# Loading the weights anew for every matmul of the modulation stage

## The chip, the cores and the metric

The kernel runs on one core of a Trainium2 chip. The metric is the device time of one execution, in microseconds (us), lower being better.

## The reference

A decode step of one transformer block for 8 sequences, one token each. The modulation is the first step: it gives six vectors of 1024 for each sequence. Attention over a cache of 8192 positions and a gated feed-forward layer follow.

```python
mod = (silu(c) @ w_mod).reshape(8, 6, 1, 1024)      # w_mod: 1024 x 6144, bf16, 12.6 MB
sa, ca, ga, sb, cb, gb = mod[:, 0], ..., mod[:, 5]
h = layernorm(x) * (1 + ca) + sa
x = x + ga * attention(h, k_cache, v_cache, wq, wo)  # K and V: 67 MB each; wq, wo: 8.4 MB each
h = layernorm(x) * (1 + cb) + sb
x = x + gb * reglu(h, W_gate, W_up, W_down)          # 7.3 MB each
```

## The kernel before

All large inputs stream through one ring in on-chip memory, in a fixed order: w_mod in two halves, wq in two halves, then K and V pieces by turns, then the rest. A load is issued as soon as the ring space that it needs has been read. The ring holds 16.8 MB, so the second half of wq needs the space of w_mod's first half, and the first K piece that of w_mod's second half. This is how the modulation can, in principle, hold up the stream.

```python
def hold(ins, when):                 # marks matmuls that shall not load weights
    if when:
        holding.append(ins)
    return ins
...
for i in range(2):                                   # the two halves of w_mod
    fns = []
    for kk in range(4 * i, 4 * i + 4):               # 8 slices of the contraction
        w = arena[:, ...]                            # [cut]
        for pr in range(3):                          # 3 pairs of output vectors
            for j in range(4):                       # 4 column tiles of the array
                fns.append(lambda e, ...: hold(e.matmul(
                    ps[32 * j:32 * j + 32, pr, :], hT[:, kk, :], w[:, 2 * pr:2 * pr + 2, j, :],
                    start=(kk == 0), stop=(kk == KC - 1), tile_position=(0, 32 * j)), pr > 0))
    P.op("pe", fns, reads=[R("hT"), slot_r(...)], writes=[bank(0, 3)])
```

The weights (the stationary operand) of all 12 matmuls of a slice are the same: `hT[:, kk, :]`, 128 rows by 32 columns. The four matmuls of a pair work side by side, each on its own 32 columns of the array; I call them a group. With `pr > 0` held, only the first group of a slice loads weights. The query projection and the gate/up matmuls hold theirs in the same way.

## Time and profile before

Median 436.92 us, 436.73 to 436.95 in three runs. The profiled execution has a span of 435.6 us.

The page's slices: each digit is the busy share, in tenths, of one of 40 equal slices of the span (10.9 us each); PEclk is the clock granted to TensorE, in tenths of full speed (below, "half clock" is 0.50); the last line is the data rate. The queue line gives packets, megabytes and the share of 16 engines' time.

```profile
PE   0415238659595958768595958768595958636437
...
PEclk9966668697888869696978969696987969668858
DMA  9999999999999999999999999999999999999995
GB/s 373 438 444 433 429 433 433 434 430 432 433 433 433 433 433 433 433 433 433 433 433 433 433 433 433 433 433 433 433 433 433 433 433 433 423 429 444 428 420 233
...
q1 hardware_dynamic: 6944, 185.61, 98.9%
```

The data engines are busy in every slice but the last, at a rate that hardly moves between the first and the last; TensorE (PE) is busy for at most half of each of the first four slices. The Trainium skill ("DMA: Bandwidth & Descriptors", Specifications) gives 435 GB/s as the ceiling of the fabric into on-chip memory; the 433 GB/s of this trace agree. The kernel is at that ceiling, so a change can make it slower only by interrupting the stream or by lengthening what follows the last data; the modulation stands at the start, where only the first can happen.

The modulation's line (L521) in the list by line: first its matmuls, then its weight loads (PEld), with count, shortest, median and longest duration in ns.

```profile
L521 PE MATMUL ps<-arena,hT x96: 378/634/635, 17.8 to 35.9; 128*32 128x512 bf16 x96
L521 PEld LDWEIGHTS ps<-arena,hT x32: 98/150/152, 17.8 to 35.1; 128*32 128x32 bf16 x32
```

The second half of the stage in the timeline (start, duration, engine, line, operation; in brackets the idle time before and what ended it), up to the first use of wq:

```profile
31.74 0.11 PEld L521 LDWEIGHTS ps<-arena,hT 128*32 128x32 bf16 x4 [10.37 <-DMA arena<-in_w_mod_dram]
31.74 4.54 PE L521 MATMUL ps<-arena,hT 128*32 128x512 bf16 x48 [9.24 <-DMA arena<-in_w_mod_dram]
32.57 0.16 PEld L521 LDWEIGHTS ps<-arena,hT 128*32 128x32 bf16 x4 [0.72 <-issue]
33.85 0.17 PEld L521 LDWEIGHTS ps<-arena,hT 128*32 128x32 bf16 x4 [1.11 <-issue]
35.13 0.16 PEld L521 LDWEIGHTS ps<-arena,hT 128*32 128x32 bf16 x4 [1.12 <-issue]
36.33 0.33 SPq L393 DMA_DIRECT2D arena<-in_A_k_cache_dram  x1
...
41.40 3.60 PE L544 MATMUL ps<-arena,hT 128*32 128x512 bf16 x32 [5.11 <-DMA arena<-in_A_wq_dram]
```

Four things are to be read here. TensorE waited 9.24 us for the data. The four loads of a slice overlap each other: four of a median 150 ns span 0.16 us. Slices follow each other every 1.28 us, which is three groups at 0.427 us. And the end of the stage releases the first K load at 36.33 us, while TensorE itself next waits 5.11 us for wq.

### The profile page before, as it was taken

How to read it: one execution, taken by the hardware profiler on the slowest of the kernel's cores; microseconds unless marked ns; L12 is line 12 of the kernel's file. 1: busy time of each engine (PE TensorE's matmuls, PEld its weight loads, DVE VectorE, ACT ScalarE, POOL GpSimd, SP SyncE). 2: the span in 40 equal slices, each digit the busy share in tenths (PEclk: the TensorE clock that was granted, in tenths of full speed). 3: DMA queues.
4: the chain of work that ended last, by engine and by line, in shares of the span. 5: the costliest groups of instructions: out<-in, count | busy, mean ns of one | idle time of the engine just before them, and what ended most of it. 6: DMA issues, size and time to landing. Idle time of an engine off the chain costs nothing.

```text
span 435.6 us, 3869 instructions
## 1 busy us (share of the span) xinstructions
PE 277.4 (64%) x1643; PEld 120.8 (28%) x1483; DVE 265.8 (61%) x377; ACT 29.9 (7%) x62; POOL 14.5 (3%) x32
## 2 busy tenths in 40 slices
PE   0415238659595958768595958768595958636437
PEld 0100002324242423324242333324142323334105
DVE  1503058777686877777778777677788776253020
ACT  2000010110101010010101010010101010110000
POOL 7000000000000000000000000000000000000000
PEclk9966668697888869696978969696987969668858
DMA  9999999999999999999999999999999999999995
GB/s 373 438 444 433 429 433 433 434 430 432 433 433 433 433 433 433 433 433 433 433 433 433 433 433 433 433 433 433 433 433 433 433 433 433 423 429 444 428 420 233
DMA packets 7078, 185.74 MB, mean 426 GB/s; under 512 B 832, under 2 KB 928, under 8 KB 1312
## 3 DMA queue, kind: packets, MB, share of 16 engines
q1 hardware_dynamic: 6944, 185.61, 98.9%
q8 instruction: 5, 0.08, 0.1%
q10 hardware_dynamic: 128, 0.04, 0.0%
q14 instruction: 1, 0.01, 0.0%
HBM read 185.63 MB, written 0.02 MB: 426 GB/s over the span
## 4 chain that ended last, share of the span: by engine, by line
PE 46%; DVE 20%; issue 13%; DMA 6%; ACT 0%; SPq 0%
PE ps L646 22%; PE ps L597 18%; DVE kt L586 9%; DMA arena<-in_B_W_down_dram 6%; DVE negm L609 5%; PE ps L615 2%; PE ps L663 2%; PE ps L743 1%; DVE om L657 1%; DVE mj L620 1%; PE ps L774 1%; DVE mjt L623 1%; DVE negm L613 1%; DVE kt L733 0%; DVE lx L706 0%
## 5 line engine op out<-in xcount | busy, mean ns | idle before, releaser
L586 DVE STREAM_TRANSPOSE kt<-arena 128x1024 uint32<-128x1024 uint32 x128 | 149.6, 1217 | 39.0 <-PE ps L597 26.8
L597 PE MATMUL ps<-kt,qpad 128*128 128x512 bf16 x512 | 122.4, 385 | 9.6 <-DVE kt L586 8.3
L646 PE MATMUL ps<-arena,pT 128*64 128x512 bf16 x512 | 95.4, 554 | 51.7 <-issue 51.7
L646 PEld LDWEIGHTS ps<-arena,pT 128*64 128x64 bf16 x512 | 45.5, 157 | 95.5 <-issue 91.1
L597 PEld LDWEIGHTS ps<-kt,qpad 128*128 128x128 bf16 x512 | 46.0, 97 | 84.6 <-DVE kt L586 28.7
L636 DVE STREAM_TRANSPOSE pT<-prb 64x1024 bf16<-64x1024 bf16 x32 | 39.6, 1239 | 18.1 <-ACT prb L629 17.6
L629 ACT ACTIVATE prb<-ps,bias 128x1024 bf16<-128x1024 f32 x16 | 17.8, 1113 | 293.1 <-DVE mjt L623 293.1
L609 DVE TENSOR_REDUCE negm<-ps 128x1 f32<-128x512 f32 x32 | 22.1, 692 | 12.7 <-PE ps L597 12.7
L663 PE MATMUL ps<-jmp,om 128*128 128x16 f32 x34 | 7.4, 293 | 17.0 <-DVE om L657 17.0
L657 DVE SCALAR_TENSOR_TENSOR om<-ps,im,om 128x128 f32<-128x128 f32 x51 | 17.7, 347 | 0.7
L615 PE MATMUL ps<-identf,negm 128*128 128x128 f32 x32 | 7.8, 326 | 15.6 <-DVE negm L613 15.6
L578 POOL TENSOR_TENSOR qpad<-qR,mq 128x128 bf16<-128x128 bf16 x16 | 6.3, 399 | 317.6 <-DVE pT L636 267.7
L774 PE MATMUL ps<-arena,hT 128*32 128x448 bf16 x128 | 9.4, 459 | 9.4 <-DMA arena<-in_B_W_up_dram 6.8
L544 PE MATMUL ps<-arena,hT 128*32 128x512 bf16 x64 | 7.1, 623 | 12.7 <-DMA arena<-in_A_wq_dram 12.7
L521 PE MATMUL ps<-arena,hT 128*32 128x512 bf16 x96 | 9.2, 565 | 9.2 <-DMA arena<-in_w_mod_dram 9.2
L793 PE MATMUL ps<-arena,hmT 128*32 128x256 bf16 x112 | 8.7, 320 | 5.6 <-DMA arena<-in_B_W_down_dram 5.4
L528 DVE COPY mod<-ps 128x512 f32<-128x512 f32 x2 | 1.3, 671 | 17.8 <-PE ps L521 17.8
L781 DVE TENSOR_TENSOR kt<-ps,kt 128x448 bf16<-128x448 f32 x2 | 1.2, 621 | 17.6 <-PE ps L774 17.6
L663 PEld LDWEIGHTS ps<-jmp,om 128*128 128x128 f32 x34 | 5.7, 210 | 20.5 <-DVE om L657 20.5
L615 PEld LDWEIGHTS ps<-identf,negm 128*128 128x128 f32 x32 | 4.7, 187 | 23.6 <-DVE negm L613 23.6
L555 DVE CAST kt<-ps 128x512 bf16<-128x512 f32 x1 | 0.7, 692 | 16.3 <-PE ps L544 16.3
L793 PEld LDWEIGHTS ps<-arena,hmT 128*32 128x32 bf16 x112 | 6.2, 114 | 9.0 <-DMA arena<-in_B_W_down_dram 7.6
(89 smaller groups left out, 89.2 us busy)
## 6 DMA issues: line engine op xcount, KB each, us to landing
arena<-in_A_k_cache_dram SPq DMA_DIRECT2D x16, 4096.0 KB, 21.1
arena<-in_A_v_cache_dram SPq DMA_DIRECT2D x16, 4096.0 KB, 19.0
arena<-in_A_wq_dram SPq DMA_DIRECT2D x2, 4096.0 KB, 34.9
arena<-in_A_wo_dram SPq DMA_DIRECT2D x2, 4096.0 KB, 18.0
arena<-in_B_W_gate_dram SPq DMA_DIRECT2D x2, 3584.0 KB, 15.5
arena<-in_B_W_up_dram SPq DMA_DIRECT2D x2, 3584.0 KB, 19.0
arena<-in_w_mod_dram SPq DMA_DIRECT2D x1, 6144.0 KB, 30.7
arena<-in_w_mod_dram SPq DMA_DIRECT2D x1, 5888.0 KB, 16.6
```

The source lines that it names most:

```text
L521: fns.append(lambda e, w=w, pr=pr, j=j, kk=kk: hold(e.matmul(ps[32 * j:32 * j + 32, pr, :], hT[:, kk, :], w[:, 2 * pr:2 * pr + 2, j, :], s ...
L586: P.op("dve", lambda e: e.transpose(ktb[:, to:to + QE].bitcast(dt.uint32), arena[:, lo:lo + QE].bitcast(dt.uint32)), reads=[slot_r(lo, lo ...
L597: fns.append(lambda e, t=t, r=r: e.matmul(ps[:, b, :].rearrange("p (c k) -> p c k", k=32), qpad[:, m % 2, t * 2 + r, 24 - 8 * i:152 - 8 * ...
L609: P.op("dve", lambda e: e.tensor_reduce(negm[:, h:h + 1], ps[:, b, :], AX.X, ALU.max, negate=True), reads=[bank(b)] + (free(("v", m - 1)) ...
L615: P.op("pe", lambda e: e.matmul(ps[:, 4, 0:128], negm[:, 2:3].to_broadcast([128, 128]), identf[:], start=True, stop=True), reads=[R("negm" ...
L629: P.op("act", lambda e: e.activation(prb[:], ps[:, 2 * z:2 * z + 2, :].rearrange("p h n -> p (h n)"), ACT.Exp, bias=bias[:, z:z + 1], scal ...
L636: P.op("dve", lambda e, g=g: e.transpose(pT[64 * g:64 * g + 64, z, :, g, :], prb[64 * g:64 * g + 64, :]), reads=[R("prb")] + ([R("qpad", z ...
L646: fns.append(lambda e, t=t: e.matmul(ps[64 * (t % 2):64 * (t % 2) + 64, 5, :].rearrange("p (i d) -> p i d", d=Dh), pT[:, z, t].rearrange(" ...
L657: P.op("dve", lambda e, i=i: e.scalar_tensor_tensor(out=om[:], in0=ps[:, 5, Dh * i:Dh * i + Dh], scalar=im[:, i:i + 1], in1=om[:], op0=ALU ...
L663: P.op("pe", lambda e: e.matmul(ps[:, 6 + z, 0:16], om[:], jmp[:].rearrange("p g j -> p (g j)"), start=True, stop=True), reads=[R("om"), R ...
L774: fns.append(lambda e, w=w, r=kk - r0, kk=kk, h=h, j=j, b0=b0: hold(e.matmul(ps[32 * j:32 * j + 32, b0 + h, 0:H], hT[:, kk, :], w[:, r, j, ...
L793: fns.append(lambda e, w=w, r=k - r0, k=k, i2=i2, j=j: e.matmul(ps[32 * j:32 * j + 32, 4, 0:256], hmT[:, k, 1 - i2:33 - i2], w[:, r, i2, j ...
```

## The change

The intent: every one of the modulation's 96 matmuls loads its weights, 64 loads more than before. Nothing else changes; on each engine the order of instructions is the same.

```diff
-                            start=(kk == 0), stop=(kk == KC - 1), tile_position=(0, 32 * j)), pr > 0))
+                            start=(kk == 0), stop=(kk == KC - 1), tile_position=(0, 32 * j)), False))
```

## The prediction

> **What bounds the kernel now.** Data movement. The page's slices show the 16 DMA engines at least 90% busy in 39 of 40 slices, mostly at 433 GB/s; the input queue alone takes 98.9% of 16 engines' span (queue table), for 185.6 MB. TensorE matmuls cover 64%, VectorE 61%. In the modulation stage (first 37 us) TensorE is mostly idle: it waits 9.2 us for the second half of w_mod (waits).
>
> **What the change does.** Each of 8 slices of the contraction does 3 output pairs x 4 column tiles of 128x512 matmuls, 96 in all. Before, only the first pair loads weights: 32 loads of 128x32 (median 150 ns; four together span 0.16 us in the timeline). After, all 96 load: 64 more loads; nothing is removed or re-ordered. The query and gate/up matmuls keep their held weights.
>
> **Cost on TensorE.** 16 more groups of four, 16 x 0.16 = 2.6 us of weight-load busy time, nearly all hidden under running matmuls:
> - In this stage a slice with its four loads takes 1.28 us, exactly three groups of 0.427 us (512 columns at half clock); the next slice's loads start beside the last group of the slice before.
> - The P x V matmuls load for every matmul, two per pair of column tiles; pairs still start 0.42 us apart at half clock, and at full clock 16 loads take 1.64 us, 0.205 us a pair: no stall.
>
> The Trainium skill ("TensorE: Matmul & The Clock Gate", Part 3) says that TensorE pulls weight loads ahead of matmuls in flight, but that they overlap only where the row group differs. Here tiles share all rows and differ in columns; the trace shows overlap all the same. If the sentence held here, a half would grow by 8 x 0.16 = 1.3 us (estimate). I expect 4.5 to 4.9 us per half (now 4.68 and 4.54), at most about 6.
>
> **How much is on the critical path.** None:
> - First half (17.8 to 22.5 us): the second half's weights land only at 31.7 us, 9.2 us of slack. Its end lets the second query-weight load be issued (22.9 us), but earlier loads occupy the queue until 41.4 us: 18 us of slack.
> - Second half (31.7 to 36.3 us): its end releases the first K load (36.3 us), with query weights in flight until 52.6 us: 16 us of slack. VectorE finishes the transposed activations at 39.0 us; the query projection waits for its own weights until 41.4 us: 2.4 us of slack, more than the pessimistic 1.3 us. Behind it lie 7.6 us more of wait, for the second half of the query weights.
>
> The stage would have to grow by about 10 us before attention started later.
>
> **Predicted time.** 436.9 us, as before; 8 in 10 between 436.4 and 437.4 (three runs before spread by 0.22 us). Chances: faster by over 2% 0.005, within 2% 0.985, slower by over 2% 0.01.
>
> **What would show it.** Weight loads rise from 1483 to 1547, on the modulation line from 32 to 96, their busy time by 2 to 4 us; the halves stay near 4.6 us; query weights land at the same times to 0.2 us; attention starts at 62.4 us; the mean stays 426 GB/s.
>
> **What would make it wrong.** If the loads drained the array between groups and a half took over 7 us, the query projection would start late, though still not the end. A different chip could shift all by some tenths. Longer TensorE code could disturb instruction fetching; the trace has 5 packets on the main instruction queue, so I count on nothing there.

## The result, and the profile after

| | before | after |
|---|---|---|
| median, us (6 runs each) | 436.95 | 436.75 |
| range, us | 436.73 to 437.04 | 436.60 to 437.10 |
| weight loads in all / on L521 | 1483 / 32 | 1547 / 96 |
| modulation, first and second half, us | 4.68, 4.54 | 5.31, 5.30 |

The ratio of after to before is 0.9997, 95% interval 0.9984 to 1.001: no difference. A ratio is the mean time of one kernel's fast runs over that of the other's of the same rounds, so it is not quite the ratio of the medians quoted.

The page's slices after:

```profile
PE   0424438668595958768595958668595958646237
...
PEclk9976658696987969698887879897878889668967
DMA  9999999999999999999999999999999999999995
GB/s 373 438 441 432 433 433 433 429 433 433 433 433 433 433 433 433 433 433 433 433 433 433 433 433 433 433 433 433 433 433 433 433 433 433 423 440 441 420 421 232
...
q1 hardware_dynamic: 6944, 185.61, 98.9%
```

The stream is as it was. The modulation's line:

```profile
L521 PEld LDWEIGHTS ps<-arena,hT x96: 98/150/151, 18.0 to 36.2; 128*32 128x32 bf16 x96
L521 PE MATMUL ps<-arena,hT x96: 606/634/635, 18.0 to 36.6; 128*32 128x512 bf16 x96
```

And the second half in the timeline:

```profile
31.93 0.14 PEld L521 LDWEIGHTS ps<-arena,hT 128*32 128x32 bf16 x8 [9.52 <-DMA arena<-in_w_mod_dram]
31.94 5.30 PE L521 MATMUL ps<-arena,hT 128*32 128x512 bf16 x48 [8.61 <-DMA arena<-in_w_mod_dram]
32.34 0.16 PEld L521 LDWEIGHTS ps<-arena,hT 128*32 128x32 bf16 x4 [0.27 <-issue]
32.77 0.16 PEld L521 LDWEIGHTS ps<-arena,hT 128*32 128x32 bf16 x4 [0.27 <-issue]
...
36.18 0.16 PEld L521 LDWEIGHTS ps<-arena,hT 128*32 128x32 bf16 x4 [0.27 <-issue]
37.29 0.33 SPq L393 DMA_DIRECT2D arena<-in_A_k_cache_dram  x1
...
43.13 3.60 PE L544 MATMUL ps<-arena,hT 128*32 128x512 bf16 x32 [5.89 <-DMA arena<-in_A_wq_dram]
```

There are now four loads before each group, and groups still start 0.43 us apart (32.34, 32.77, ...), as before. Yet the half took 5.30 us and not 4.54, and the K load went out 0.96 us later. Adding up the groups explains the number: 12 x 0.427 = 5.12 us plus the end of the last matmul is a half run wholly at half clock, while 4.54 us is less than that, so a part of it ran faster. The attention's first cache transpose starts at 62.55 us, before at 62.38.

So two questions are left although the time did as foretold. Did the loads make the halves longer? And is the stage really so far from mattering as I reckoned?

**Theory A:** loads cost nothing, being hidden under running matmuls; the halves differ because the array's clock is released at different moments. The Trainium skill ("TensorE: Matmul & The Clock Gate", Part 1) says that the clock is set by activity in a window that is free-running, so that the moment of release varies from run to run (the clock records, read below, agree). **Theory B (rival):** each added group of loads costs 0.05 to 0.16 us, or holds the clock low, and only the slack hides it.

### The profile page after: what moved, and what is told of

The parts are those of the page before. It is cut to its first block, busy times and chain, and to the rows that moved or that the text cites. A ratio compares the mean times of both kernels' runs of the same rounds, so it can differ in the third digit from the quotient of the medians.

```text
span 435.8 us, 3933 instructions
## 1 busy us (share of the span) xinstructions
PE 277.1 (64%) x1643; PEld 122.2 (28%) x1547; DVE 265.8 (61%) x377; ACT 29.9 (7%) x62; POOL 14.5 (3%) x32
## 4 chain that ended last, share of the span: by engine, by line
PE 47%; DVE 20%; issue 13%; DMA 5%; ACT 0%
PE ps L646 22%; PE ps L597 18%; DVE kt L586 9%; DVE negm L609 5%; DMA arena<-in_B_W_down_dram 5%; PE ps L793 2%; PE ps L615 2%; PE ps L663 2%; PE ps L743 1%; DVE om L657 1%; DVE mj L620 1%; PE ps L774 1%; DVE mjt L623 1%; DVE negm L613 1%; DVE kt L733 0%
## 5 line engine op out<-in xcount | busy, mean ns | idle before, releaser
L521 PE MATMUL ps<-arena,hT 128*32 128x512 bf16 x96 | 10.6, 632 | 8.6 <-DMA arena<-in_w_mod_dram 8.6
L544 PE MATMUL ps<-arena,hT 128*32 128x512 bf16 x64 | 7.2, 631 | 12.0 <-DMA arena<-in_A_wq_dram 12.0
```

Of the source, the lines that this page charges most:

```text
L521: fns.append(lambda e, w=w, pr=pr, j=j, kk=kk: hold(e.matmul(ps[32 * j:32 * j + 32, pr, :], hT[:, kk, :], w[:, 2 * pr:2 * pr + 2, j, :], s ...
```

## The experiments

All outputs are right. In kernels with dummy matmuls the dummies stand on L527, and later lines of the program are numbered 6 higher (the query projection is L550); in the kernels with 128-column matmuls the modulation is L522.

### Both kernels once more

Edit: none.

> The kernel before once more, for a second profile. The change's profile has both halves of the modulation at 5.3 us where the profile before had 4.68 and 4.54. Theory A (the added loads are hidden; the halves differ because the array's clock was released at another moment of a window that runs on its own): the halves of this unchanged kernel also vary between about 4.4 and 5.35 us from profile to profile, groups of four start 0.427 us apart at half clock. Theory B (the loads cost about 0.05 to 0.16 us per added group, or keep the clock low): the halves stay at 4.5 to 4.7 us here.

> The changed kernel once more. Theory A: groups start 0.427 us apart while the clock is at half, and the halves may come out anywhere between 4.4 and 5.35 us. Theory B: the halves stay at 5.3 us. Time 436.9 us in both.

Measured: 437.10 and 436.76 us, beside 437.17 us for a run of the kernel before. The kernel before, its two halves:

```profile
17.91 5.07 PE L521 MATMUL ps<-arena,hT 128*32 128x512 bf16 x48
...
31.86 4.92 PE L521 MATMUL ps<-arena,hT 128*32 128x512 bf16 x48 [8.87 <-DMA arena<-in_w_mod_dram]
```

The changed kernel:

```profile
17.74 4.11 PE L521 MATMUL ps<-arena,hT 128*32 128x512 bf16 x48
...
31.64 5.31 PE L521 MATMUL ps<-arena,hT 128*32 128x512 bf16 x48 [9.79 <-DMA arena<-in_w_mod_dram]
```

The same program's half varies by 0.4 us (before: 4.54 to 4.92 in the second half) and by 1.2 us (after: 4.11 to 5.31 in the first). The shortest half of all four profiles has the added loads, and at 4.11 us it lies below the 4.4 us that I had put down. Lengths alone do not refute Theory B, since an early release could hide a fixed cost. The clock settles it. In windows of the second half, before and after (window, its length, busy times of PE and PEld, clock, share of the DMA engines, GB/s), it rises between 35.0 and 35.5 us before, and only after 37.0 us with the change:

```profile
35.00:35.50 0.50, 0.50 (x12) 0.16 (x4) 0.62 0.00 0
35.50:36.00 0.50, 0.50 (x16) 0.00 (x0) 1.00 2.27 983
...
36.50:37.00 0.50, 0.50 (x8) 0.00 (x0) 0.50 0.45 197
37.00:37.50 0.50, 0.24 (x4) 0.00 (x0) 0.90 2.03 852
```

The clock records of the kept traces put the two releases of each profile at 21.72 and 35.38 us (before), 22.60 and 36.25 (before, again), 23.45 and 37.10 (after), 20.49 and 37.56 (after, again). Take groups 0.427 us apart until then, half of that afterwards, 0.17 us for the end of the last matmul, and nothing for loads. The sums are 4.68 and 4.55, 5.07 and 4.93, 5.29 and 5.29, 4.11 and 5.29 us; measured were 4.68 and 4.54, 5.07 and 4.92, 5.31 and 5.30, 4.11 and 5.31. So the release explains every half to 0.02 us and leaves no room for Theory B's cost per group. The two releases of a profile lie 13.66 us apart, or 17.07 in the last, which are 4 and 5 times 3.41 us: a step that runs on by itself, with or without the added loads. In both halves of the change's first profile the release came after the last group had started; as far as these runs tell, that was chance.

### The halves at full clock

Edit, to both kernels: 40 groups of dummy matmuls, weights held, results thrown away, after the first half, so that the array comes warm to the second.

```diff
+            if i == 0:
+                for g in range(40):
+                    for j in range(4):
+                        fns.append(lambda e, w=w, j=j, kk=kk: hold(e.matmul(
+                            ps[32 * j:32 * j + 32, 5, :], hT[:, kk, :], w[:, 0:2, j, :],
+                            start=True, stop=True, tile_position=(0, 32 * j)), True))
```

> Kernel before plus 40 groups of four dummy matmuls (held weights, results thrown away) after the first half of the modulation, so that TensorE is busy until about 31 us and the second half runs at full clock. Both theories: the second half takes 12 x 0.213 + about 0.2 = 2.6 to 2.8 us. The end does not move (436.9 us), since the release of the second query-weight load slips only from 22.9 to about 31 us, before the queue runs dry at 41.4 us.

> The same dummies in the changed kernel. Theory A: the second half takes 2.6 to 2.8 us, as with held weights, because four loads span 0.11 to 0.16 us and a group of matmuls 0.213 us. Theory B: the loads add to each of the 8 groups that held their weights, 8 x 0.1 to 0.16 = 0.8 to 1.3 us, so 3.4 to 4.1 us. The end does not move in either.

Measured: 437.01 and 436.81 us. With all loads, the second half ran at full clock:

```profile
32.53 2.77 PE L521 MATMUL ps<-arena,hT 128*32 128x512 bf16 x48 [1.53 <-DMA arena<-in_w_mod_dram]
```

The kernel with held weights missed its aim: w_mod landed at 33.36 us, 2.56 us after the dummies, the clock fell to half at 34.50 us, 1.1 us into the half, and the half took 4.25 us:

```profile
33.36 4.25 PE L521 MATMUL ps<-arena,hT 128*32 128x512 bf16 x48 [2.56 <-DMA arena<-in_w_mod_dram]
33.80 0.11 PEld L521 LDWEIGHTS ps<-arena,hT 128*32 128x32 bf16 x4 [0.34 <-issue]
34.45 0.11 PEld L521 LDWEIGHTS ps<-arena,hT 128*32 128x32 bf16 x4 [0.54 <-issue]
```

Its length can't be compared, but the slice before the fall can: 0.65 us for three groups, two of them held (33.80 to 34.45), 0.216 each, and in the kernel with all loads the trace has the groups 0.216 us apart too. A whole half with held weights came from a later experiment (the early slip, below), where dummies lead straight into it:

```profile
42.66 2.76 PE L521 MATMUL ps<-arena,hT 128*32 128x512 bf16 x48
```

At full clock: 2.77 us with 48 loads, 2.76 us with 16. The 32 added loads make a difference of 0.01 us. Theory B expected 0.8 to 1.3 us more.

### Matmuls a quarter as long

If loads are hidden under 512-column matmuls, shorter ones may uncover them. Edit: each matmul cut into four of 128 columns, weights held as before in one kernel (32 loads), loaded for each in the other (384). The diff is cut: it leaves out the rest of each call, with the flags that hold weights.

```diff
-                    for j in range(4):
-                        ... ps[32 * j:32 * j + 32, pr, :], hT[:, kk, :], w[:, 2 * pr:2 * pr + 2, j, :], ...
+                    for q in range(4):
+                        for j in range(4):
+                            ... ps[32 * j:32 * j + 32, pr, 128 * q:128 * q + 128], hT[:, kk, :],
+                                w[:, 2 * pr + q // 2, j, 128 * (q % 2):128 * (q % 2) + 128], ...
```

The accumulation's start flag: only the first of the four sets it.

> The modulation's matmuls cut into four of 128 columns each (384 in place of 96), weights held but for the first group of each slice as in the kernel before: 32 loads. The array's work is the same, so a half takes 5.1 us at half clock (48 groups x 0.107), less when the clock is released, unless matmuls this short are bound by issue. End unmoved.

> The same cut, every matmul loading its weights: 384 loads. Four loads span 0.11 to 0.16 us, a group of four 128-column matmuls 0.107 us at half clock and 0.053 at full. If a load needs its own time once matmuls are too short to cover it: 48 x 0.11 to 0.16 = 5.3 to 7.7 us per half, and the clock does not matter much. If loads were free at any size: as with held weights. End unmoved in either case (436.9 us), as the halves have 9 and 10 us of slack.

Measured: 436.89 and 437.10 us. Held: halves of 4.09 and 4.14 us, both partly at full clock. With 384 loads:

```profile
18.02 5.04 PEld L522 LDWEIGHTS ps<-arena,hT 128*32 128x32 bf16 x192
18.02 5.23 PE L522 MATMUL ps<-arena,hT 128*32 128x128 bf16 x192
...
32.98 4.10 PE L522 MATMUL ps<-arena,hT 128*32 128x128 bf16 x153 [9.72 <-DMA arena<-in_w_mod_dram]
39.47 0.74 PE L522 MATMUL ps<-arena,hT 128*32 128x128 bf16 x39 [2.39 <-issue]
```

48 groups at half clock are 48 x 0.107 = 5.1 us, and the first half took 5.23: even here loads add nothing that shows, although weights are being loaded nearly all the time (5.04 us). Nor do they at full clock: in the second half, from the clock's release at 36.69 us to the pause below, groups with four loads each start 0.056 us apart (three intervals, and six in the repeat), as do the held groups of the other kernel at full clock. My expectation of 5.3 to 7.7 us erred to the high side: the 0.16 us span of four loads is a latency, not the interval at which the array can take the next four.

The second half shows something new: a pause of 2.39 us that waits for nothing the profile shows. This kernel has 7 packets on the main instruction queue, the kernel before 5 and the one with held weights 6. I ran it again:

> The 384-load kernel again. Its first profile showed a pause of 2.4 us within the second half, put down to issue, and 7 instruction packets against 5 before. If it comes from fetching the longer code, it recurs at the same matmul (after 153 of the half's 192), with 7 packets; if it was chance, the half takes 5.1 us or less with no pause. End unmoved in either case.

Measured: 436.98 us; 153 matmuls in 3.92 us, a pause of 2.56 us, then 39; 7 packets. The pause recurs at the same matmul, so it belongs to the program and not to chance. That it is the fetching of longer code fits the packets, but I did not test it apart, and packets alone do not bring it: the kernel with 141 groups of dummies (below) has 7 as well and runs them without a pause, though at four instructions per 0.217 us where this one has eight per 0.056 to 0.107. It did not reach the end either.

### How far the stage can slip: second half

Edit: the dummies of above after the second half (`if i == 1`), 47, 94 and 141 groups, added to the kernel before. They delay the release of the first K load and everything after the modulation.

> Kernel before plus 47 groups of four dummy matmuls at the end of the second half of the modulation: TensorE finishes it about 10 us later (47 x 0.213), so the first K load is issued at about 46 instead of 36.3 us. Theory A (slack of 16 us until the queue runs dry at 52.6 us): the time stays at 436.9 us within 0.5. Rival (the early stage is on the critical path, its delay passes on): about 447 us.

> 94 groups, about 20 us later: the first K load is issued at about 56 us, after the queue has run dry at 52.6 us and with about 2 us until data flow again. Theory A: 4 to 6 us longer, 441 to 443 us, with one dip in the DMA rate near 53 to 58 us. Rival: 457 us.

> 141 groups, about 30 us later: past the slack each us costs a us. Theory A: 10 us more than with 94 groups, 451 to 453 us. Rival: 467 us.

| kernel | first K load issued, us | median, us | ratio (95%) | longer by, us | issue minus loss, us |
|---|---|---|---|---|---|
| before | 36.33 | 436.91 | | | |
| 47 groups | 46.85 | 436.87 | 0.9999 (0.9984 to 1.0015) | 0.0 | |
| 94 groups | 57.15 | 445.40 | 1.0196 (1.0181 to 1.0212) | 8.5 | 48.7 |
| 141 groups | 67.14 | 455.36 | 1.0423 (1.0407 to 1.0439) | 18.5 | 48.7 |

Ten microseconds of delay cost nothing that shows (the interval is about 0.7 us either way); the rival (delay passes on in full) is refuted. Beyond a point, each microsecond costs one: from 94 to 141 groups the issue moves 9.99 us and the time 9.96. But the break is at 48.7 us (issue minus loss, the same from both runs), not where I had put it: the slack is 48.7 - 36.3 = 12.4 us, not 16, and the losses were above what I expected (4 to 6, 14 to 16). The windows of the 94-group kernel show why. The columns are the window, its length, busy times of PE, PEld, DVE, ACT and POOL, clock, share of the DMA engines, and GB/s (a packet counts whole where it starts, so a short window's share can exceed 1):

```profile
48.00:50.00 2.00, 2.00 (x44) 0.00 (x0) 0.00 (x0) 0.00 (x0) 0.00 (x0) 1.00 0.80 344
50.00:52.00 2.00, 2.00 (x44) 0.00 (x0) 0.00 (x0) 0.00 (x0) 0.00 (x0) 1.00 0.08 25
...
56.00:58.00 2.00, 1.11 (x24) 0.00 (x0) 0.81 (x2) 0.60 (x1) 0.00 (x0) 1.00 0.00 0
58.00:60.00 2.00, 0.04 (x4) 0.07 (x4) 1.90 (x5) 0.00 (x0) 0.00 (x0) 1.00 0.92 262
```

And of the 47-group kernel:

```profile
50.00:52.00 2.00, 2.00 (x24) 0.57 (x12) 0.38 (x2) 0.00 (x0) 0.00 (x0) 0.50 1.18 508
```

Without a K load in the queue, data ran out at about 50 us; with it they flow on. I had taken 52.6 us, when the second half of wq lands in the kernel before, for the moment at which the queue runs dry. But a load lands with its last packet, and the engines do not finish together. By the packet records of the 94-group trace, the packets in flight fall from 16 at 50.00 us to 3 at 50.50, and the last two end at 51.9, with no K load behind them to share the engines. K data sharing them can thus account only for the rest, 51.9 to 52.6 us.

The same records balance the loss: each engine was idle for 7.8 us on average, and the first 16 packets then took 1.83 us on average instead of 1.21, 8.4 us together for 8.5 lost. The first packet starts 0.97 us after the issue; I had allowed about 2 us until data flow here, and nothing in the prediction.

### How far the stage can slip: first half

Edit: 94 groups after the first half. This tests the corrected reckoning on another load, the second half of wq.

> Kernel before plus 94 groups of four dummy matmuls after the first half of the modulation: the second query-weight load is issued at about 42.9 instead of 22.9 us. The earlier slips showed that 41.4 or 52.6 us, when a load lands, is not when the queue runs dry. Rule from them, tested here on the other load: without the later load the queue ran dry at 50.1 us, and 4.19 MB less at 433 GB/s make it 40.4 us; 1.6 us from issue to data. Rule: 42.9 + 1.6 - 40.4 = 4.1 us longer, 441.0 us (440.2 to 441.8), with one dip in the DMA rate near 40 to 45 us. Rival (my prediction's reckoning, slack 18 us up to the landing at 41.4 us): 42.9 - 41.4 = 1.5 us longer, 438.4 us. Second half of the modulation at full clock: 2.8 us.

Measured: 440.56 us against 437.10, ratio 1.0079 (1.0062 to 1.0096), 3.5 us longer, clear of noise. The load was issued at 42.87 us, and data had all but run out by 41:

```profile
40.00:41.00 1.00, 1.00 (x28) 0.00 (x0) 0.00 (x0) 0.00 (x0) 0.00 (x0) 1.00 0.14 49
41.00:42.00 1.00, 1.00 (x24) 0.00 (x0) 0.00 (x0) 0.00 (x0) 0.00 (x0) 1.00 0.00 0
42.00:43.00 1.00, 1.00 (x24) 0.10 (x4) 0.00 (x0) 0.00 (x0) 0.00 (x0) 1.00 0.00 0
43.00:44.00 1.00, 1.00 (x28) 0.20 (x8) 0.00 (x0) 0.00 (x0) 0.00 (x0) 1.00 1.17 328
```

The rule (441.0, range 440.2 to 441.8) held; the reckoning by landing times (438.4) did not. The remaining 0.6 us is within the interval (0.7 us). The packet records give 40.8 us for the mean end of the engines' work where I had 40.4, and 0.94 us from issue to first packet where I had 1.6, but the first packets were again 0.6 us slower than later ones. The true slack of the first half is 42.87 - 3.46 - 22.54 = 16.9 us (22.54 is the issue in the kernel before), where I had said 18.

### No held weights anywhere

Edit: the changed kernel with `z > 0` (query projection) and `h > 0` (gate/up) made `False` as well: 1643 loads, none held.

> The changed kernel with the query projection and the gate/up matmuls loading anew as well, so no held weights anywhere: 32 + 64 more loads, 1643 in all. Theory A: these stages too wait for their weights from memory, and their loads hide under matmuls: 436.9 us within 0.5. Rival (held weights matter where TensorE runs near the end): up to 1 us longer, from the last gate/up parts.

Measured, in five rounds: 436.92 us against 436.91, ratio 1.0001 (0.9987 to 1.0015). Its modulation halves took 4.69 and 4.56 us, as short as in the first profile of the kernel before, with three times the loads. Holding weights is worth nothing here that five rounds resolve (0.6 us either way), in all stages together.

## Why the prediction was right or wrong, point by point

- **The time.** Right: 436.75 us for 436.9 foretold.
- **What bounds the kernel.** Right, and shown: the rate stays at the fabric's ceiling in both profiles, and only the kernels that let the queue run dry became slower, by about as long as it was dry and 0.6 us for the slower first packets.
- **The loads are hidden.** Right: groups start 0.43 us apart with and without loads, and at full clock the half takes 2.77 or 2.76 us. The skill's sentence that loads overlap with matmuls in flight only where the row group differs does not hold here: all these tiles share all rows. (The same part also lets loads run ahead into a background weight buffer; no run here tells whether that is what happened.)
- **"I expect 4.5 to 4.9 us per half".** Wrong in the change's profile (5.31 and 5.30), within the bound of 6. The step that failed is that I took one profile's halves for constants. They contain the moment at which the clock is released. The unchanged kernel gave 4.54 to 5.07 us in two profiles, the changed one 4.11 to 5.31. The clock records explain each of these halves to 0.02 us without any cost of loads, and the kernel without any held weights (4.69, 4.56; released at 21.70 and 35.35 us) is as short as the first profile before. That the change's first profile came out at 5.3 us twice was the luck of the release.
- **"18 us of slack" and "16 us of slack".** The mechanism was right (the end of each half releases a load, with a full queue before it), the sizes were not: 16.9 and 12.4 us. The term that was mis-sized is the moment the queue runs dry, which I read from landing times (41.4 and 52.6 us; the engines' work ends at a mean of 40.8 and 50.5); and the restart, 0.9 to 1.0 us from issue to first packet and 0.6 for slower first packets, was left out. With no time lost, the right call needed neither size: any slack over 1 us gave the same answer.
- **The query projection's 2.4 us of slack.** The kernel with 47 groups starts the query projection at 49.66 us, 8 us late, and the time does not change. This slack was thus never critical.
- **"Query weights land at the same times to 0.2 us".** Wrong for the first half of wq (41.40 before, 43.13 after), right for the second (52.63 and 52.79). The wait for the first half ended between 41.40 and 43.13 us over the profiles, also in kernels with held weights (42.55 in the 128-column one). What sets it stays open; nothing waited for it that mattered.
- **Busy time of the added loads.** Right: 1.21 us on L521 before, 3.48 after, 2.3 more (2 to 4 foretold). **Attention at 62.4 us:** 62.55. **426 GB/s:** unchanged.
- **Longer code and instruction fetching.** Not seen in the change (5 packets on the main queue in both; 1 and 2 on another, and 1 again in the second profile after), but the 384-load kernel has a pause of 2.4 to 2.6 us that may be this.

## What to carry to other kernels

Before crediting or fearing a change in an engine's work, ask which transfer its end releases and when the queue before that transfer would run dry; here 12 us of delay were free, and each one beyond cost its full length. Read that moment from the bytes queued and the rate, or from a slip experiment, and not from when a transfer lands, since its last packets can land well after most engines have run dry (51.9 against 50.5 us here). And take the spacing of matmuls, not the length of a stage, to compare two profiles: the clock's release alone moved the stage by up to 1.2 us.

## What the Trainium skill lacked or had wrong

- "TensorE: Matmul & The Clock Gate", Part 3, says in its list that weight loads overlap with matmuls in flight only when the row group differs; the paragraph above that list also allows it for loads into the background weight buffer. Here all tiles share all rows and differ in columns, and 48 loads among 48 matmuls made a difference of 0.01 us (2.77 against 2.76 us at full clock); 192 loads among 192 matmuls of 128 columns also fitted into 5.23 us at half clock. The list's sentence can't be used alone.
- The same page, section LDWEIGHTS, gives a load as columns / 1.2 ns, which makes 27 ns for 32 columns (estimate). The trace shows 98 to 152 ns each, four together in 0.10 to 0.17 us. Neither number is a cost per group: at full clock a group every 0.056 us carried four loads. For an ordinary load the section has one figure, and does not tell its duration from the interval to the next.
- "DMA: Bandwidth & Descriptors", Specifications, gives about 358 GB/s as the limit from memory to one core, without its condition, which the page has further down (both cores of a pair streaming). This kernel runs on one core and read 185.6 MB at a mean of 426 GB/s, 433 GB/s in most slices.
- The same table's first-byte latency of about 0.6 us does not say from where it counts. Here the first packet started 0.94 to 0.97 us after the start of the issuing instruction in three traces, which is 0.61 to 0.64 us after its end.
- No page that I found gives a time between a queue's running dry and the landing of its last transfer: here 13 of 16 engines were done by 50.5 us, and the last packet ended at 51.9.
- No page that I found says that a trace can lack clock records at its start: in the kernel before the first is at 21.72 us, and until then the clock column stands at 1.00 while groups start 0.43 us apart, the spacing of the half clock.
- "Runtime: NRT & Kernel Launch", Instruction fetch mechanics, has no time for a fetch that is not hidden; the pause of 2.4 and 2.6 us at the same matmul in two runs may be one, but its cause was not tested apart.
